# Neighbourhood attention on one Trainium2 core: the order of the opening's transfers

## The chip, the cores and the metric

The kernel runs on one core of one Trainium2 chip. The metric is the device time of one execution in microseconds (us); the time of a kernel is the median of several runs.

## The reference

An image of 224 x 224 positions with 192 channels is projected to queries, keys and values. Every position attends to a 7 x 7 neighbourhood with dilation 2, clipped at the image's edges, with one head of 192 channels. The result is projected by `wo`.

```python
def reference(x, wqkv, wo):
    B, H, W, C = x.shape          # 1, 224, 224, 192, bfloat16
    ks, dil = (7, 2)
    qkv = x @ wqkv
    q, k, v = ...                 # C channels each
    half = (ks - 1) // 2 * dil
    r0 = jnp.clip(ir - half, 0, H - 1 - (ks - 1) * dil)
    c0 = jnp.clip(ic - half, 0, W - 1 - (ks - 1) * dil)
    ...                           # nidx: the 49 neighbours r0 + 2a, c0 + 2b of each position
    logits = jnp.einsum('bnc,bnkc->bnk', qf, kn) * C ** (-0.5)
    p = softmax(logits)
    o = jnp.einsum('bnk,bnkc->bnc', p, vn) @ wo
    return o.reshape(B, H, W, C)
```

## The kernel before, in words

**Two parities, fourteen bands, 28 steps.** With dilation 2 even and odd rows never meet, nor do even and odd columns. A row parity is called `rc`, a column parity `cc`. The image is cut into bands of 16 rows. A step (`rc`, `j`) handles eight query rows of one parity. The steps are run in the order (0,0), (0,1), (1,0), (0,2), (1,1), (0,3) and so on; `si` counts them from 0. A step has seven groups, `t` = 0 to 6.

**Folding.** Queries are not formed by themselves. The product of the query and key weights is folded once at the start, and `g_piece` (L353, L361) applies it to the query rows of a step, in three pieces (kinds 0, 1, 2), into `ga` and `gb`. The value weights are folded with the output weights in the same way: `w_transpose(2, wv, 0)` (L231) transposes the value weights, and `fold_wo` (L243, L244, L269) multiplies them with the output weights into `WP`. So the attention sums raw input rows, and `o_mm` (L447) applies `WP` at the end.

**Three copies of the input.** `load_xt` (L92) brings a band as a transposed copy `xt`, in four parts of four rows, by DMA transposes that SP issues. `key_copy` (L277, L279) rearranges it into the keys `xa` and `xb`; `edge_item` (L295, L303) computes what is special at the image's left and right edge, and `edge_copies` (L329 to L332) puts that into `ga` and `gb`. `load_xn` (L105) brings the rows a second time, not transposed, as values `xn`: one DMA for each of 14 column tiles `n`, band and row parity, into 64 partitions. Two consecutive bands fill the 128 partitions; an even band is in the lower half. `grp_copy` (L208, L210) fills fixed columns beside each value tile, used by one of the two y products.

**A group.** `s_group` (L410, L411) forms scores of four tiles, ACT takes the exponential (L414), and `y_unit` (L429, L435) multiplies the probabilities with value tiles, in pairs of units for a column parity and a half, (`cc`, `h`); the half `h` = 1 uses tiles 7 to 13, and `h` = 0 the tiles from 0 up. `Y0` says in which group of step 0 each unit runs. `o_mm` and `o_out` (L447, L451, L462) of the step before are run between. The order on every engine is written out by hand, as the program's order.

**What step 0 needs.** Step 0 uses band 0 alone. Its groups 3, 4 and 5 form the pieces of step 1, which need parts 0, 1 and 2 of band 1; group 6 runs the edge item of band 1. Step 1 forms the pieces of step 2, of bands 0 and 1; step 2 those of step 3, of bands 1 and 2.

**Queues.** SP issues its transfers in the order of the program. In the program's instructions every transfer that SP issues waits for the end of the eighth one before it (the first weights, issued by ACT, count as the first), and POOL's likewise among themselves. `gate` (L216) is a copy of one element on POOL: it holds back what POOL issues behind it until a given part of a band has landed. `DOWN` is the list of tiles from 13 to 0. Before the change SP issues band 0, two parts of band 1, the value and output weights (L113 to L115), part 2, three value tiles, part 3, seven value tiles of band 1, band 2, and five value tiles of the second parity; POOL issues the other value tiles in one sequence.

Of the kernel before, what the change touches and what calls it, by code (L numbers as in the profile page):

```python
# [17 lines left out]
KC = 8  # L18
QW = KC + HALO
NEG = -30000.0  # L20
XP = 448
# [6 lines left out]
def kernel(  # L28
# [7 lines left out]
    nc = tc.nc  # L36
# [3 lines left out]
    NJ = H // 16  # L40
# [43 lines left out]
    xt = {}  # L84

    def load_xt(b, part):
        if not 0 <= b < NJ:
            return
        if b not in xt:
            xt[b] = xt_pool.tile([128, 3, 16, S], BF, name=f"xt{b}", tag="xt")  # L90
        r = 4 * part
        nc.sync.dma_start_transpose(out=xt[b][:, :, r:r + 4, :].rearrange("p t r c -> p t (r c)"),  # L92
                                    in_=xp[16 * b + r:16 * b + r + 4].rearrange("r j c -> (r j) c"))

    NX = 11
    DOWN = list(range(NK - 1, -1, -1))

    def load_xn(eng, rc, m, tiles):

        if not 0 <= m < NJ:  # L100
            return
        p0 = 64 * (m % 2)
        r0 = 16 * m + rc
        for n in tiles:
            eng.dma_start(out=XN[rc][p0:p0 + 64, XP * n + 64:XP * (n + 1)],  # L105
                          in_=xp[r0:r0 + 15:2, KC * n:KC * (n + 1), :])

    nc.scalar.dma_start(out=wqk[:], in_=wqkv[:, 0:2 * C].rearrange("(a p) c -> p a c", p=CH))
    for part in range(4):
        load_xt(0, part)  # L110
    for part in range(2):
        load_xt(1, part)
    nc.sync.dma_start(out=wv[:], in_=wqkv[:, 2 * C:3 * C].rearrange("(a p) c -> p a c", p=CH))  # L113
    nc.sync.dma_start(out=wo_lo[:], in_=wo[0:128, :])
    nc.sync.dma_start(out=wo_hi[:], in_=wo[64:192, :])  # L115
    load_xt(1, 2)
    load_xn(nc.sync, 0, 0, DOWN[NX:])
    load_xt(1, 3)
    load_xn(nc.sync, 0, 1, DOWN[:7])
    for part in range(4):  # L120
        load_xt(2, part)
    load_xn(nc.sync, 1, 1, DOWN[:5])


    i_id = const.tile([128, 128], I32, name="i_id")
# [75 lines left out]
    def masks(eng, gi, ccs=(0, 1)):  # L201
        for cc in ccs:
            g = GB[gorder[gi] + (cc,)]
            eng.tensor_copy(out=g[CROW[cc]], in_=cmE[CROW[cc]])
            eng.tensor_copy(out=g[RROW[cc]], in_=rm[RROW[cc], gi, :].unsqueeze(1).to_broadcast([32, S, BR]))

    def grp_copy(eng, rc):
        eng(out=XN[rc][:, 0:NK * XP].rearrange("p (n c) -> p n c", c=XP)[:, :, 0:64],  # L208
            in_=grp[:].unsqueeze(1).to_broadcast([128, NK, 64]))
        eng(out=XN[rc][:, NK * XP:], in_=grp[:])  # L210
# [3 lines left out]

    gate = const.tile([1, 1], BF, name="gate")
    nc.gpsimd.tensor_copy(out=gate[:], in_=xt[0][0:1, 0, 12, 0:1])  # L216
    load_xn(nc.gpsimd, 0, 0, DOWN[:NX])


    def filler(n):  # L220
# [5 lines left out]
    def w_transpose(X, src, c0):  # L226
        pool_, tag = (ps_y, "y") if X < 2 else (ps_s, "s")
        tp = pool_.tile([128, 2, 2, CH], BF, name="tp" + tag, tag=tag)
        for i, d0 in enumerate((0, 64)):
            for a in range(2):  # L230
                nc.tensor.transpose(tp[:, i, a, :], src[:, a, c0 + d0:c0 + d0 + 128], ident[0:CH, 0:CH])  # L231
        f = "p a b -> p (a b)"
        nc.scalar.copy(out=wT_lo[:, X, PAD:PAD + C], in_=tp[:, 0].rearrange(f))
        nc.scalar.copy(out=wT_hi[64:128, X, PAD:PAD + C], in_=tp[64:128, 1].rearrange(f))
# [29 lines left out]
    def fold_wo():  # L264
        for kt, cs in enumerate(((64, 0), (-64, 128))):
            pt = ps_y.tile([128, 2, 256], F32, name="prW", tag="y")
            for cc in range(2):
                times(pt[:, cc, 0:C], 2, cs[cc], wo_lo[:], wo_hi[:])
            nc.scalar.copy(out=WP[:, :, kt, 0:C], in_=pt[:, :, 0:C])  # L269
# [118 lines left out]

    yplan = [(0, 1, (2, 3)), (0, 0, (4, 5)), (1, 1, (6, 7)), (1, 0, (8, 8))]
    HS = ((0, H0), (H0, S))  # L390
    Y0 = {(0, 1): (4, 5), (0, 0): (6, 6), (1, 1): (7, 7), (1, 0): (8, 9)}

    class Step:
        pass
# [137 lines left out]
    for si, st in enumerate(steps):  # L532
        rc, j = st.rc, st.j
        prev = steps[si - 1] if si else None
        nxt = steps[si + 1] if si + 1 < len(steps) else None
        st.ysb = [work.tile([128, 2, NO, 128], BF, name=f"ysb{cc}", tag=f"ysb{cc}", bufs=2) for cc in range(2)]

        for (cc, h, ts) in yplan:
            for kt in range(2):
                pend.append((si * T + (ts[kt] if si else Y0[cc, h][kt]), st, cc, h, kt))  # L540
        up = None if si < 2 else (prev.rc, prev.j + 1 + prev.rc)
        if up:
            key_copy(*up, 0, nc.vector.tensor_copy, nc.vector.tensor_copy)
        for t in range(T):
            s_group(st, t)
            if t == (6 if si == 1 else 3) and rc == 0 and 2 <= j + 1 < NJ:
                edge_item(j + 1)
            if si == 0:
                if t == 0:
                    rest(nc.vector.tensor_copy)  # L550
                    g_piece(0, 0, 2)
                    edge_item(0)
                    key_copy(0, 0, 1, nc.vector.tensor_copy, nc.vector.tensor_copy)
                    load_xn(nc.gpsimd, 0, 1, DOWN[7:])
                    load_xn(nc.gpsimd, 1, 0, DOWN[:7])
                    load_xn(nc.gpsimd, 1, 1, DOWN[5:7])
                    load_xn(nc.gpsimd, 1, 0, DOWN[7:])
                    load_xn(nc.gpsimd, 1, 1, DOWN[7:])
                elif t == 1:
                    edge_copies(0, 0, nc.vector)  # L560
                    masks(nc.vector, 2)
                elif t == 2:
                    for cc in range(2):
                        onehots(nc.vector, cc, 1)
                        key_copy(1, 0, cc, nc.vector.tensor_copy, nc.vector.tensor_copy)
                elif t < 6:
                    if t == 3:
                        w_transpose(2, wv, 0)
                    if t == 4:
                        fold_wo()  # L570
                    g_piece(nxt.rc, nxt.j, t - 3)
                else:
                    edge_item(1)
                    edge_copies(nxt.rc, nxt.j, nc.vector)
            elif t < 3 and nxt is not None:
                g_piece(nxt.rc, nxt.j, t)
            if prev is not None:
                tp_ = t - (3 if nxt is not None else 2)
                if 0 <= tp_ < 4:
                    o_out(*o_mm(prev, PIECES[tp_]))  # L580
            run_y(si * T + t)
            if t == (0 if si > 2 else 2) and si > 0 and nxt is not None:
                edge_copies(nxt.rc, nxt.j, nc.gpsimd if si > 1 else nc.vector)
            if up and t == 0:
                load_xn(nc.sync, *up, (12, 11))
                load_xn(nc.gpsimd, *up, (10, 9, 8))
            elif up and t == 1:
                load_xn(nc.gpsimd, *up, (13, 7, 6, 5, 4, 3, 2, 1, 0))
            if nxt is None and t == 4:
                store(prev, [nc.sync, nc.gpsimd], parts=(1, 2))  # L590
            if nxt is None and t == 6:
                first = o_mm(st, (0, 1, 2, 3), (0,))
            if t == 5 and up:
                key_copy(*up, 1, nc.scalar.copy, nc.vector.tensor_copy)

            if si == 1 and t in (0, 2, 4, 5):
                load_xt(3, (0, 2, 4, 5).index(t))
            elif si > 1 and t in (1, 4):
                load_xt(j + (4 if rc else 2), 2 * (rc == 0) + (t == 4))
            if si == 0 and t in (4, 5):  # L600
                key_copy(0, 1, t - 4, nc.vector.tensor_copy, nc.vector.tensor_copy)
            if si == 1:
                if t == 1:
                    masks(nc.vector, 1)
                    grp_copy(nc.scalar.copy, 1)
                if t in (0, 2):
                    key_copy(1, 1, t // 2, nc.vector.tensor_copy, nc.vector.tensor_copy)
            if si > 1 and held and t in (1, 2, 3, 5, 6):
                (nc.sync if t in (2, 5) else nc.gpsimd).dma_start(**held.pop(0))
            if t == 2 and si in (2, 3, 8):  # L610
                masks(nc.vector, {2: 4, 3: 3, 8: 5}[si])
        if prev is not None:
            if si == 1:
                store(prev, None, later=held)
            elif nxt is not None:
                store(prev, [nc.sync])
            else:
                store(prev, [nc.sync, nc.gpsimd], parts=(0, 3), cols=(0, NO))
# [63 lines left out]
```

## Time and profile before

| | |
|---|---|
| median of 3 runs | 328.31 us (328.27 to 328.81) |
| profiled execution | 327.94 us, of which the span is 326.2 us |
| granted TensorE clock, mean | 0.984 |
| busy: PE, DVE, ACT, POOL | 94%, 83%, 76%, 66% of the span |
| moved by DMA | 59.02 MB, 181 GB/s on average |
| first scores of steps 1 and 2 | 28.94 and 41.90 us |

Times in the views count from the span's start. PE is TensorE, PEld its weight loads, DVE VectorE, ACT ScalarE, POOL GpSimd, SP the engine that issues most transfers. A line of a timeline has the start, the duration, the engine, the line of the kernel, what is written and read, and in square brackets how long the engine was idle before and what released it.

### The profile page before, as it was taken

To read this page: it belongs to the slowest core of one execution; us is meant where nothing else is said; L and a number is where in the kernel's file an instruction comes from. 1 tells how busy PE (TensorE), PEld (TensorE's weight loads), DVE (VectorE), ACT (ScalarE), POOL (GpSimd) and SP (SyncE) were. 2 spreads that over 40 slices of the span, in tenths; PEclk is the share of its full clock that TensorE was granted. 3 is DMA by queue.
4 is the path that set the end of the run, shared out by engine and by line. 5 is a ranking of instruction groups with operands and counts; after the bars stand their busy time and mean duration, and the time that the engine had idled before them with its cause. 6 is when DMAs were issued, how large, how long until landed. Compare 5 with 4: busy or idle time off the path is not lost.

```text
span 326.2 us, 12220 instructions
## 1 busy us (share of the span) xinstructions
PE 307.6 (94%) x4978; PEld 270.6 (83%) x4978; DVE 269.3 (83%) x538; ACT 246.9 (76%) x516; POOL 214.6 (66%) x442
## 2 busy tenths in 40 slices
PE   7859999999999999999999999999999999999980
PEld 6537888988889888988899888988899888988980
DVE  8838989988978989888988898788988898887771
ACT  5636777788887787878888787878787887888651
POOL 2768657989766866776668667676567866753052
PEclk9969999999999999999999999999999999999997
DMA  8999999899888999999989998999999943644233
GB/s 162 183 171 179 215 164 220 184 225 225 186 204 209 212 148 199 224 212 210 202 183 205 217 182 161 226 213 184 213 193 207 214 118 105 171 134 124 59 103 97
DMA packets 106319, 59.02 MB, mean 181 GB/s; under 512 B 92945, under 2 KB 100315, under 8 KB 106263
## 3 DMA queue, kind: packets, MB, share of 16 engines
q1 hardware_dynamic: 89479, 40.73, 65.3%
q0 software_dynamic: 16576, 17.37, 22.6%
q8 instruction: 39, 0.64, 0.8%
q10 hardware_dynamic: 208, 0.15, 0.2%
q14 instruction: 17, 0.14, 0.1%
HBM read 19.59 MB, written 19.27 MB: 119 GB/s over the span
## 4 chain that ended last, share of the span: by engine, by line
PE 73%; DVE 14%; SPq 4%; issue 3%; DMA 3%; ACT 1%; POOL 0%; POOLq 0%; DVEq 0%; ACTq 0%
PE y L429 19%; PE po L447 15%; PE pg L353 14%; PE s_ps L410 9%; PE s_ps L411 9%; DVE o_sb L462 6%; PE pg L361 4%; SPq L92 3%; DVE ysb L435 3%; DMA xt<-in_x_dram 2%; PE pe L295 1%; DVE rs L451 1%; DVE gb L367 1%; DVE gb L370 1%; DMA xn<-in_x_dram 1%
## 5 line engine op out<-in xcount | busy, mean ns | idle before, releaser
L105 POOL DMA_DIRECT2D xn<-in_x_dram x329 | 184.8, 587 | 77.0 <-PE y L429 46.0
L414 ACT ACTIVATE p_sb<-s_ps 128x448 bf16<-128x448 f32 (+3 forms) x196 | 105.6, 539 | 20.5 <-PE s_ps L411 20.2
L429 PE MATMUL y<-p_sb,xn 128*128 128x112 bf16 (+5 forms) x1736 | 108.0, 207 | 0.1
L429 PEld LDWEIGHTS <-xn 128*128 128x128 bf16 (+1 forms) x1736 | 95.3, 97 | 13.0 <-issue 6.1
L435 ACT CAST ysb<-y 128x504 bf16<-128x504 f32 (+1 forms) x140 | 73.2, 544 | 35.3 <-PE y L429 32.3
L410 PE MATMUL s_ps<-ga,xa 128*128 128x112 bf16 (+4 forms) x812 | 98.9, 210 | 0.8 <-DVE xa L277 0.5
L411 PE MATMUL s_ps<-gb,xb 128*128 128x112 bf16 (+4 forms) x812 | 98.5, 210 | 0.5 <-DVE gb L330 0.4
L462 DVE TENSOR_TENSOR o_sb<-po,rs 128x768 bf16<-128x768 f32 x109 | 93.5, 858 | 5.3 <-DVE rs L451 0.9
L447 PE MATMUL po<-WP,ysb 128*128 128x193 bf16 x770 | 82.7, 247 | 1.8 <-ACT ysb L435 0.6
L411 PEld LDWEIGHTS <-xb 128*128 128x128 bf16 (+1 forms) x812 | 76.2, 98 | 0.7 <-issue 0.3
L410 PEld LDWEIGHTS <-xa 128*128 128x128 bf16 (+1 forms) x812 | 72.9, 98 | 2.3 <-issue 1.2
L447 PEld LDWEIGHTS <-ysb 128*128 128x128 bf16 x784 | 62.6, 98 | 3.6 <-ACT ysb L435 1.9
L353 PE MATMUL pg<-xt,wz 128*128 128x327 bf16 (+3 forms) x336 | 51.5, 289 | 4.7 <-DMA xt<-in_x_dram 4.6
L435 DVE CAST ysb<-y 128x392 bf16<-128x392 f32 (+1 forms) x84 | 49.6, 591 | 0.9 <-PE y L429 0.7
L451 DVE RECIPROCAL rs<-po 128x4 f32<-128x4 f32 x110 | 19.3, 175 | 21.0 <-PE po L447 19.4
L367 DVE CAST gb<-pg 64x872 bf16<-64x872 f32 x27 | 28.6, 1058 | 7.8 <-PE pg L361 6.9
L353 PEld LDWEIGHTS <-wz 128*128 128x128 bf16 x336 | 24.5, 98 | 12.6 <-issue 4.2
L365 ACT CAST ga<-pg 128x872 bf16<-128x872 f32 x28 | 24.8, 885 | 11.8 <-PE pg L353 11.8
L370 DVE CAST gb<-pg 64x848 bf16<-64x848 f32 x28 | 29.3, 1045 | 0.4
L375 ACT CAST ga<-pg 128x848 bf16<-128x848 f32 x28 | 24.2, 865 | 0.6 <-PE pg L353 0.6
L279 DVE COPY xb<-xt 64x896 bf16<-64x896 bf16 x56 | 23.0, 411 | 0.8
L277 ACT COPY xa<-xt 128x896 bf16<-128x896 bf16 x24 | 22.6, 940 | 0.0
(88 smaller groups left out, 176.7 us busy)
## 6 DMA issues: line engine op xcount, KB each, us to landing
xn<-in_x_dram POOLq DMA_DIRECT2D x329, 48.0 KB, 4.4
out_dram<-o_sb SPq DMA_DIRECT2D x25, 630.0 KB
xn<-in_x_dram SPq DMA_DIRECT2D x63, 48.0 KB
xt<-in_x_dram SPq DMA_TRANSPOSE x56
out_dram<-o_sb SPq DMA_DIRECT2D x50, 9.0 KB
out_dram<-o_sb POOLq DMA_DIRECT2D x9, 78.8 KB, 4.3
out_dram<-o_sb SPq DMA_DIRECT2D x7, 78.8 KB
out_dram<-o_sb SPq DMA_DIRECT2D x25, 18.0 KB
```

Source lines behind the costliest of these rows:

```text
L105: eng.dma_start(out=XN[rc][p0:p0 + 64, XP * n + 64:XP * (n + 1)], in_=xp[r0:r0 + 15:2, KC * n:KC * (n + 1), :])
L353: nc.tensor.matmul(pg[:, a_:b_, 0:nq], lhsT=AW[w], rhs=xt[b][:, k, la:la + 2 * (b_ - a_ - 1) + 1:2, q0:q0 + nq], start=(a_ == ra if kind = ...
L365: nc.scalar.copy(out=A[0][:, 3:S, :], in_=pg[:, :, 0:nq].rearrange(v))
L367: mid(out=Bt[0][0:64, 3:S, :], in_=pg[0:64, :, 0:nq].rearrange(v))
L370: mid(out=Bt[1][64:128, HALO:S, :], in_=pg[64:128, :, 3:nq].rearrange(v))
L410: nc.tensor.matmul(o, lhsT=XA[rc][:, cc, n, 0:kn], rhs=a[:, lo:hi, :].rearrange(f), start=True, stop=False)
L411: nc.tensor.matmul(o, lhsT=XB[cc][rc][:, n, 0:kn], rhs=b_[:, lo:hi, :].rearrange(f), start=False, stop=True)
L414: nc.scalar.activation(out=p[0:kn, 0:off], in_=s_ps[0:kn, 0:off], func=ACTF.Exp)
L429: nc.tensor.matmul(y[:, BR * (a_ - h0):BR * (b_ - h0)], lhsT=XN[st.rc][kp, d:d + 128], rhs=p[kp, off + BR * (a_ - lo):off + BR * (b_ - lo) ...
L435: eng(out=o, in_=y[:, 0:BR * (h1 - h0)].rearrange("p (i n r) -> p i n r", n=NO, r=BR))
L447: nc.tensor.matmul(po[:, k, 0:C + 1], lhsT=st.ysb[cc][:, kt, n, :], rhs=WP[:, cc, kt, 0:C + 1], start=(kt == 0), stop=(kt == 1))
L462: nc.vector.tensor_tensor(out=o, in0=po[:, 0:k, 0:C], in1=rs[:, 0:k].to_broadcast([128, k, C]), op=ALU.mult)
```

## The change

SP issues all four parts of band 1 behind band 0. The value rows of six tiles are then loaded for both bands at once by `load_both`, one DMA into 128 partitions, and only then the weights of values and output; after them band 2 and four tiles of the second parity, again for two bands at once. POOL loads eight tiles of band 0, eight of band 1, waits for the first part of band 2, and loads ten tiles of the second parity for two bands at once. Transposing and folding the output weights go from groups 3 and 4 of step 0 to groups 0 and 1 of step 1. The edge item of band 2 goes from group 6 of step 1 to group 1 of step 2. The first y unit of step 0 goes from group 4 to group 5, beside the second. The `grp_copy` of the second parity goes from group 1 to group 5 of step 1.

```diff
+    def load_both(eng, rc, tiles):
+        for n in tiles:
+            eng.dma_start(out=XN[rc][:, XP * n + 64:XP * (n + 1)], in_=xp[rc:rc + 31:2, KC * n:KC * (n + 1), :])
...
-    for part in range(2):
+    for part in range(4):
         load_xt(1, part)
+    load_both(nc.sync, 0, DOWN[8:])
     nc.sync.dma_start(out=wv[:], in_=wqkv[:, 2 * C:3 * C].rearrange("(a p) c -> p a c", p=CH))
     nc.sync.dma_start(out=wo_lo[:], in_=wo[0:128, :])
     nc.sync.dma_start(out=wo_hi[:], in_=wo[64:192, :])
-    load_xt(1, 2)
-    load_xn(nc.sync, 0, 0, DOWN[NX:])
-    load_xt(1, 3)
-    load_xn(nc.sync, 0, 1, DOWN[:7])
     for part in range(4):
         load_xt(2, part)
-    load_xn(nc.sync, 1, 1, DOWN[:5])
+    load_both(nc.sync, 1, DOWN[10:])
...
-    load_xn(nc.gpsimd, 0, 0, DOWN[:NX])        # NX = 11
+    load_xn(nc.gpsimd, 0, 0, DOWN[:8])
...
-    Y0 = {(0, 1): (4, 5), (0, 0): (6, 6), (1, 1): (7, 7), (1, 0): (8, 9)}
+    Y0 = {(0, 1): (5, 5), (0, 0): (6, 6), (1, 1): (7, 7), (1, 0): (8, 9)}
...
-            if t == (6 if si == 1 else 3) and rc == 0 and 2 <= j + 1 < NJ:
+            if (si, t) == (2, 1):
+                edge_item(2)
+            if t == 3 and rc == 0 and 3 <= j + 1 < NJ:
                 edge_item(j + 1)
...                                            # step 0, group 0
-                    load_xn(nc.gpsimd, 0, 1, DOWN[7:])
-                    load_xn(nc.gpsimd, 1, 0, DOWN[:7])
-                    load_xn(nc.gpsimd, 1, 1, DOWN[5:7])
-                    load_xn(nc.gpsimd, 1, 0, DOWN[7:])
-                    load_xn(nc.gpsimd, 1, 1, DOWN[7:])
+                    load_xn(nc.gpsimd, 0, 1, DOWN[:8])
+                    nc.gpsimd.tensor_copy(out=gate[:], in_=xt[2][0:1, 0, 0, 0:1])
+                    load_both(nc.gpsimd, 1, DOWN[:10])
...                                            # step 0, groups 3 to 5
-                    if t == 3:
-                        w_transpose(2, wv, 0)
-                    if t == 4:
-                        fold_wo()
                     g_piece(nxt.rc, nxt.j, t - 3)
...                                            # later steps, groups 0 to 2
+                if (si, t) == (1, 0):
+                    w_transpose(2, wv, 0)
+                if (si, t) == (1, 1):
+                    fold_wo()
                 g_piece(nxt.rc, nxt.j, t)
...                                            # step 1
                 if t == 1:
                     masks(nc.vector, 1)
+                if t == 5:
                     grp_copy(nc.scalar.copy, 1)
```

## Prediction

> **What bounds the kernel now.** I read the page first, then the opening through the chain of waits, TensorE's timeline, the windows and the queues. In the page, PE is busy for 94% of the span; the two weak places are the first and the last slices.
>
> ```profile
> PE   7859999999999999999999999999999999999980
> PEclk9969999999999999999999999999999999999997
> DMA  8999999899888999999989998999999943644233
> ```
>
> Slice 3 (16.3 to 24.5 us) is the only place before the tail where PE is half idle and its granted clock falls; DMA is full from the start. The chain of waits, restricted to 12 to 24 us, says which transfer:
>
> ```profile
> 11.63 0.43 SPq L114
> 12.06 0.04 issue
> 12.11 0.43 SPq L115
> 12.54 0.04 issue
> 12.58 7.33 DMA xt<-in_x_dram
> ```
>
> Columns are start, duration, what. SP issues the two copies of the output weights, then band 1's part 2, which lands 7.33 us later, at 19.91. TensorE's timeline shows who waits, and the windows what its clock does:
>
> ```profile
> 15.38 0.34 PE L231 MATMUL tps<-ident,wv 96*128 96x96 bf16 x4
> 15.56 0.54 PE L353 MATMUL pg<-xt,wz 128*128 128x327 bf16 x4
> 19.95 0.89 PE L353 MATMUL pg<-xt,wz 128*128 128x436 bf16 x2 [3.85 <-DMA xt<-in_x_dram]
> ...
> 15.23:18.64 3.41, 0.87 (x11) 0.53 (x9) 3.34 (x9) 1.05 (x3) 2.34 (x4) 1.00 1.08 132
> 18.64:22.06 3.42, 2.10 (x13) 1.23 (x13) 0.62 (x2) 1.18 (x2) 2.70 (x6) 0.51 1.26 195
> 22.06:25.47 3.41, 3.41 (x25) 2.14 (x24) 0.69 (x1) 1.23 (x4) 2.18 (x5) 0.50 0.80 163
> ```
>
> In a window line the first "us, (x)" pair is PE, and the three figures at the end are clock, DMA share, GB/s. PE idles 3.85 us; the clock is 1.00 to 18.64, then half until 25.47, two stretches of 3.41 us. VectorE waits with it, and later becomes the bound itself:
>
> ```profile
> 24.77 1.06 DVE L367 CAST gb<-pg 64x872 bf16<-64x872 f32 x1 [5.50 <-PE pg L361]
> 32.45 1.06 DVE L367 CAST gb<-pg 64x872 bf16<-64x872 f32 x1
> ```
>
> From 32.45 the chain runs on DVE to 41.21, and later again. Both were released by PE, so an earlier PE moves this chain too. After 70 us no wait of PE on a DMA appears among its waits and its steps are about 11 us, nearly all busy: what the opening gains should reach the end.
>
> **DMA prices.** A half tile of value rows (48 KB): page section 3 has q0 move 17.37 MB in 22.6% of 326.2 us, 4.24 us a MB, so 0.21 us. A both-band tile is counted twice that, 0.42. A part of a band (344 KB transposed): q1's 65.3% are 213 us for 40.73 MB; 21.4 MB of that are stores and straight loads, 91 us at q0's price, leaving 122 us for 56 parts, 2.2 us each. Bounds: band 0's four parts landed at 10.32 (POOL's gate), of which about 2.0 are start and 0.6 the first weights, hence 1.93; and part 2 to part 3 of band 1 took 3.84 us (19.91 to 23.75, when SP's queue ends its 0.9 us wait), beside three half tiles from SP and about 4.5 from POOL, hence 2.27. The three later weight transfers have 448 rows of 384 bytes; the first weights took 0.6 us with 208 packets, so 1.3 us; the rest of the wait for part 3 (10.32 to 23.75, less 4 x 2.2 and 14 x 0.21) bounds it above by 1.7.
>
> **Part 2 earlier.** In the changed order it has no weights ahead: 10.32 + 3 x 2.2 + five POOL half tiles (POOL's lane waits show about one landing per us from 12 on) x 0.21 = 18.0 (17.1 to 18.4). PE arrives 0.18 earlier, as the value-weight transposes are gone from this spot, so it idles about 2.1 us instead of 3.85.
>
> **The clock.** The stretch to 18.64 would be 0.7 + 0.6 = 1.3 of 3.41 busy, 38%. Before it was 26% and the clock fell; a stretch at 68% (315.65 to 319.07) kept it. 38% lies nearer to 26%, so I take a fall, and because the next stretch is full, recovery at 22.06: half the former penalty. The Trainium skill ("TensorE: Matmul & The Clock Gate", HAM oscillation) says instead that only idle gaps over about 3.4 us matter; the trace disagrees in part, for the fall came 2.5 us after PE's last matmul. By that rule there would be no fall, PE would reach the next data 1.7 us sooner, and the early-tile rival below would follow.
>
> **Rest of step 0.** From 19.95 to step 1's first scores at 28.94 PE did 5.52/2 + 3.47 = 6.2 us of full-clock work; without the folding (21.66 to 22.92 at half clock, 0.63) 5.6. The last 0.9 is the pair of y units of (0,0), now the first users of the tiles that SP loads for both bands. From 18.0 PE gets there at 22.7 at full clock, at 24.4 with the fall. y of (0,1), moved a group later, needs POOL's first seven half tiles; the seventh lands by about 20.5, PE gets there at 20.8: free. The edge item needs part 3: 18.0 + 2.2 + 0.6 = 20.8, free too.
>
> **Tile 0** is the last of SP's six both-band tiles and the first that y of (0,0) reads. After part 3: 6 x 0.42, and about six POOL half tiles beside it, 1.3: 24.6. Bounds: 22.1 with 1.93 per part and three half tiles, 26.2 with 2.27 and all sixteen of POOL's landed. SP's issue is no limit: part 3 ends its issue near 14.3, six issues at 0.65 end near 18.3, and each waits for the eighth transfer before it, the last for band 1's part 1. So y of (0,0) starts at 24.6 whichever way the clock goes, and step 1 at 25.5 instead of 28.94: 3.4 earlier.
>
> **Moved work.** Value-weight transposes (0.18) and folding (0.63) now run in step 1's first two groups: +0.8 on PE. Behind them on PE wait the key-map pieces, which feed the DVE chain. The weights land behind tile 0 at 25.2 to 26.0; PE asks for them at 26.0 and 28.3: covered, and worth up to 1 if not. ACT's four copies (0.30, 0.31, 0.48, 0.48) come where the two group copies of the second parity (0.94, 0.25) leave; those go to group 5, where ACT had idle of 0.4 to 0.8 us per group. The folding shares the y banks, whose evictions fall before it: zero, bound 0.5. The step-1 edge item (0.46 on PE, 0.47 on DVE) goes to step 2, and with it the 0.55 wait that followed (40.71 to 41.26, on a normalization freeing its bank); DVE is nearly full in step 2 too, so I count half: -0.3, bounds 0 and -0.6.
>
> **Queues behind.** POOL's new gate waits for band 2's part 0 (tile 0 at 24.6, weights 1.3, 2.2, a little POOL: about 28.5); behind it stand ten both-band tiles of the second parity. At POOL's 0.57 us an issue (1.1 if it grew with the partitions) the seventh goes out at 32.5 (36.2) and lands 5 us later, 37.5 (41); step 2's first y, at 46.56 before, comes near 43.7. Band 2's part 3 lands at 28.5 + 3 x 2.2 + up to 4.2 = 35 to 39; DVE's key copy, at 42.75 before, comes near 39.9. Both covered, the second closely. Fewer DMA instructions (20 tiles at double width) shorten only issue queues: nothing.
>
> Sum: -3.4 + 0.8 - 0.3 = -2.9 on the profiled 327.94, 325.0. The median of before is 0.37 above that execution, so 325.4. About 0.2% (0.66 us) is what a measurement tells from no change.
>
> **Rivals.**
> Tiles early: if tile 0 lands near 22.7 and the clock holds, step 1 starts at 23.6; -5.3 + 0.8 - 0.3 = -4.8, 323.5. For it: DMA shares of 1.2 to 1.5 in 12 to 20 us show overlap that my unit prices omit. Against: it needs the low end of two bounds and an untested clock. 0.14.
> The stall moves: all transfers share the same engines, already full (share 0.8 to 1.6 from 4 us on), so what is postponed is late next. Counting to the end of the second parity's first tiles: 12 x 2.2 + 56 x 0.21 + 0.6 + 1.3 + 2.0 = 42.1, beside up to four parts of band 3; step 2's second y pair comes at about 46. A stall there, or at the key copy, of 1 to 2 us leaves a gain near 1.4: 326.9. The Trainium skill ("DMA: Bandwidth & Descriptors", Issuing engines are not separate DMA queues) says of sharing what these rows show. 0.16.
> Nothing: part 2 lands at 19.9 as before, the weights having filled gaps; then only small shifts remain, 328.2. 0.06.
> Slower: the clock holds at 18.64, PE reaches y of (0,0) at 22.7, and tile 0 comes only at 27. PE is then idle 2.8 of the 3.41 us to 25.47, the clock falls there, stays half through the partly idle next stretch to 28.88 and up to 32.3. The two y units end at 28.8, and 1.75 us are lost to the slow clock; with +0.8 and -0.3 that is 28.8 - 28.9 + 1.75 + 0.5 = +2.1, 330.4. It decides from tile 0 at about 26, my upper bound. 0.14, with unknown waits of this kind.
>
> **Numbers.** Forecast 0.50, as above, its own range 324.0 to 326.3. Faster: 0.50 + 0.14 + 0.16 = 0.80; same 0.06; slower 0.14. The range leaves out the slower case and the ends of the others: 323.2 to 328.2.
>
> **What would show it.** Right: PE's wait for band 1 ends near 18; half clock for one stretch or none before 23; a wait of y on value rows near 24.6; step 1's scores at 25.5; L367 of step 1 about 2.4 us earlier than 32.45; no PE wait on DMA later. Wrong: part 2 landing after 19, tile 0 after 26, a clock fall at 25.47, or a DVE key copy waiting for band 2 in step 2.

## Result: 1.1% slower, though TensorE finishes earlier

The changed kernel takes 331.75 us (median of six runs, 330.52 to 332.29) beside 328.18 us of the kernel before (six runs, 327.5 to 328.81): a ratio of 1.0106, 95% interval 1.0083 to 1.0129. The forecast was 325.4. The profiled execution took 332.1 us with a span of 330.2 us; before, 327.94 and 326.2.

The opening first. From the page of the changed kernel, the rows of PE, its granted clock and DMA over 40 slices:

```profile
PE   7779999999999999999999999999999999999930
PEclk9979999999999999999999999999999999999985
DMA  9999999989998999999998889989898654442350
```

The weak third slice has become better on PE. At the other end PE's slice 39 has fallen from 8 to 3, though its work is the same: the span goes on for longer after TensorE has stopped. The chain of waits of the changed kernel (start, duration, what), its PE timeline and its windows at the places that the prediction showed:

```profile
9.51 1.66 SPq L92
11.17 0.04 issue
11.21 7.65 DMA xt<-in_x_dram
```

```profile
18.91 0.92 PE L354 MATMUL pg<-xt,wz 128*128 128x436 bf16 x2 [2.80 <-DMA xt<-in_x_dram]
...
25.25 1.22 PE L430 MATMUL y<-p_sb,xn 64*128 64x112 bf16 x16
26.40 0.20 PE L411 MATMUL s_ps<-ga,xa 128*128 128x64 bf16 x1
...
26.93 0.92 PE L354 MATMUL pg<-xt,wz 128*128 128x436 bf16 x6
```

```profile
15.51:18.92 3.41, 0.61 (x8) 0.33 (x6) 3.34 (x9) 0.54 (x1) 1.25 (x2) 1.00 1.24 158
18.92:22.33 3.41, 3.41 (x21) 1.69 (x22) 0.42 (x2) 1.42 (x2) 3.21 (x6) 0.50 1.13 281
22.33:25.74 3.41, 3.41 (x58) 2.69 (x56) 3.21 (x5) 2.21 (x4) 0.11 (x1) 1.00 1.21 209
```

Part 2 of band 1 has no weights ahead of it and lands at 18.9, so PE idles 2.80 us instead of 3.85. The clock is half for one stretch (18.92 to 22.33) instead of two. The y products of (0,0) at 25.25 have no bracket: they wait for no value rows. Step 1's first scores come at 26.40, 2.5 us earlier. VectorE's key-map copy of step 1, which began at 32.45 before:

```profile
31.46 1.06 DVE L368 CAST gb<-pg 64x872 bf16<-64x872 f32 x1 [1.43 <-PE pg L362]
```

Of the 2.5 us, 1.0 is left here. From step 2 on, the second piece of each step starts 1.3 to 1.6 us earlier than before, to the last; ACT's last work ends at 318.26 instead of 319.66, and the last store lands at 322.22 instead of 323.94.

So the whole loss, and more, lies behind the last landing. There each engine ends with DRAIN instructions, and POOL's longest DRAIN, called the drain below, is what changes. The instructions of the program's last line (engine, operation, count: shortest, median and longest in ns, first and last start), before and after:

```profile
L677 POOLq DRAIN  x3: 40/102/4627, 320.5 to 325.9; - x3
L677 SPq DRAIN  x3: 7/7/13, 325.3 to 325.7; - x3
```

```profile
L679 POOLq DRAIN  x3: 40/102/10308, 319.1 to 330.0; - x3
L679 SPq DRAIN  x3: 7/7/13, 323.4 to 329.7; - x3
```

And SP's waits between 300 us and the end (us in total, times, longest), before and after:

```profile
SPq L677 <- DMA out_dram<-o_sb: 3.2, 3, 2.6
SPq L677 <- PEq L677: 0.7, 2, 0.5
```

```profile
SPq L679 <- PEq L679: 6.7, 2, 6.2
SPq L679 <- DMA out_dram<-o_sb: 2.6, 3, 1.6
```

Before, SP's last long wait is for the stores. After, it has seen the stores land and waits 6.2 us more for the other engines at the common end (the view puts PE's name to it; PE's own drains last 1.3 us at most, and the late one is POOL's). POOL's drain takes 10.31 us instead of 4.63. It ends 7.2 us after the last store has landed, instead of 1.2. The account: the landing 1.7 us earlier, the drain's end 6.0 us later behind it, 4.3 in all, of which the span shows 4.0 (326.2 to 330.2).

### The profile page after: what moved, and what is told of

The parts are those of the page before. It is cut to its first block, busy times and chain, and to the rows that moved or that the text cites. A ratio compares the mean times of both kernels' runs of the same rounds, so it can differ in the third digit from the quotient of the medians.

```text
span 330.2 us, 12196 instructions
## 1 busy us (share of the span) xinstructions
PE 307.4 (93%) x4978; PEld 270.2 (82%) x4978; DVE 269.6 (82%) x538; ACT 247.0 (75%) x516; POOL 205.4 (62%) x428
## 4 chain that ended last, share of the span: by engine, by line
PE 73%; DVE 14%; SPq 3%; issue 3%; DMA 2%; ACT 1%; POOL 0%; POOLq 0%; DVEq 0%; ACTq 0%
PE y L430 19%; PE po L448 16%; PE pg L354 14%; PE s_ps L411 9%; PE s_ps L412 9%; DVE o_sb L463 5%; PE pg L362 4%; SPq L92 3%; DVE ysb L436 2%; DMA xt<-in_x_dram 2%; PE pe L296 1%; DVE gb L368 1%; DVE gb L371 1%; DVE rs L452 1%; DVE gb L205 1%
## 5 line engine op out<-in xcount | busy, mean ns | idle before, releaser
L104 POOL DMA_DIRECT2D xn<-in_x_dram x304 | 170.4, 588 | 75.9 <-PE y L430 42.1
L354 PE MATMUL pg<-xt,wz 128*128 128x327 bf16 (+3 forms) x336 | 51.6, 289 | 4.1 <-DMA xt<-in_x_dram 4.1
L354 PEld LDWEIGHTS <-wz 128*128 128x128 bf16 x336 | 24.4, 98 | 12.2 <-DMA xt<-in_x_dram 3.7
L368 DVE CAST gb<-pg 64x872 bf16<-64x872 f32 x27 | 28.6, 1058 | 6.3 <-PE pg L362 5.5
```

What stands on the lines that cost most here:

```text
L354: nc.tensor.matmul(pg[:, a_:b_, 0:nq], lhsT=AW[w], rhs=xt[b][:, k, la:la + 2 * (b_ - a_ - 1) + 1:2, q0:q0 + nq], start=(a_ == ra if kind = ...
L368: mid(out=Bt[0][0:64, 3:S, :], in_=pg[0:64, :, 0:nq].rearrange(v))
```

## Experiments

The change takes 15 transfers off POOL (352 become 337): ten tiles for two bands replace twenty half tiles, and five go to SP. The experiments ask what of this makes the drain long. "Transfers" below are those that POOL issues.

### Form or count: halves, before_337, after_352

`halves` is the changed kernel with the ten both-band tiles of POOL as twenty half tiles again (347 transfers):

```diff
-                    load_both(nc.gpsimd, 1, DOWN[:10])
+                    load_xn(nc.gpsimd, 1, 0, DOWN[:10])
+                    load_xn(nc.gpsimd, 1, 1, DOWN[:10])
```

> The changed kernel, but POOL loads the ten tiles of the second parity as twenty half tiles (64 partitions each), so that no POOL transfer has 128 partitions; POOL issues 347 transfers in all (changed kernel 337, before 352). Theory 'form': the 10.3 us of POOL's last DRAIN comes from the 128-partition transfers; then the drain falls to about 4.6 us and the time to about 326.5. Theory 'count': the drain follows the number of POOL transfers; it changes with 347, to a value not known beforehand. Theory 'gate': the second copy on POOL between transfers is what is paid; drain stays near 10 us, time 332.

`before_337` is the kernel before, with fifteen half tiles of steps 8 to 14 issued by SP instead of POOL; `after_352` is the changed kernel with fifteen of steps 8 to 15 issued by POOL instead of SP:

```diff
-                load_xn(nc.sync, *up, (12, 11))
-                load_xn(nc.gpsimd, *up, (10, 9, 8))
+                few = {8: 3}.get(si, 2 if 9 <= si <= 14 else 0)          # before_337
+                load_xn(nc.sync, *up, (12, 11) + (10, 9, 8)[:few])
+                load_xn(nc.gpsimd, *up, (10, 9, 8)[few:])
...
+                more = {8: 1}.get(si, 2 if 9 <= si <= 15 else 0)         # after_352
+                load_xn(nc.sync, *up, (12, 11)[more:])
+                load_xn(nc.gpsimd, *up, (12, 11)[:more] + (10, 9, 8))
```

> The kernel before, with 15 half tiles of steps 8 to 14 issued by SP instead of POOL: POOL issues 337 transfers, as in the changed kernel, but all in the old form and with the old opening. 'Count': drain near 10.3 us and a time near 333.5, slower than before by over 5 us though nothing else changes. 'Form' and 'gate': drain stays at 4.6 us, time 328.

> The changed kernel, with 15 half tiles of steps 8 to 15 issued by POOL instead of SP: POOL issues 352 transfers, as before. 'Count': drain back at 4.6 us and the time near 326.5, faster than before by 1.4 to 1.9. 'Form' and 'gate': drain stays near 10 us, time 332.

Measured: `halves` has a drain of 4.18 us and takes 326.54 us, 0.9945 of before (0.9916 to 0.9974), as theory 'form' had it. But `after_352` keeps the both-band tiles and has a drain of 4.50 us; its time, 327.74 us, 0.9995 (0.9966 to 1.0025), misses the 326.5 that 'count' expected. `before_337` has the old opening and a drain of 10.31, 338.66 us, 1.0315 (1.0252 to 1.0378). So the form of the transfers does not do it, nor the new opening; the number does something. `before_337` was a poor instrument for the price: it also lost 7 to 8 us between 139 and 209 us, where PE waited up to 2.65 us at a time for value rows, now partly from SP's queue. Right behind the longest of these waits the granted clock was half for one stretch (167.8 to 171.2 us).

### Neither the second gate nor the program's length: nogate, pad_337

`nogate` takes the second `gate` copy out of the changed kernel. `pad_337` puts fifteen one-element writes on POOL at the start:

```diff
-                    nc.gpsimd.tensor_copy(out=gate[:], in_=xt[2][0:1, 0, 0, 0:1])      # nogate
...
+    for _ in range(15):                                                                # pad_337
+        nc.gpsimd.memset(gate[:], 0.0)
```

> The changed kernel without the copy on POOL that waits for band 2's first part, so that POOL issues the second parity's tiles without that wait; 337 transfers. 'Gate': drain back to 4.6 us, time near 326.5, or more if the tiles now delay band 2. 'Count' and 'form': drain near 10 us, time 332 or more.

> The changed kernel with fifteen one-element memsets more on POOL, where it waits for band 0 anyway: 337 POOL transfers, but as many POOL instructions (448) as the 352-transfer kernel. If the drain follows the number of transfers it stays at 10.31 us and the time near 331.5. If it follows the length of POOL's program it falls to about 4.5 us and the time to about 326.

Both keep a drain of 10.31 us: 331.38 us, 1.0126 (1.0083 to 1.0169), and 331.49 us, 1.0108 (1.0063 to 1.0153). The gate, which the prediction had looked at for what stands behind it, costs nothing that these runs show.

### A wrong turn: a remainder, a threshold, an event

`after_338` and `after_353` move one and sixteen half tiles from SP to POOL, by the edit of `after_352`; `after_327` has SP issue the ten held stores (stores of the opening's results, which POOL otherwise issues in steps 2 and 3); `after_342` moves five half tiles to POOL.

```diff
-                (nc.sync if t in (2, 5) else nc.gpsimd).dma_start(**held.pop(0))
+                nc.sync.dma_start(**held.pop(0))                                       # after_327
```

> The changed kernel with one half tile of step 8 on POOL instead of SP: 338 transfers, 434 instructions. A threshold between 337 and 347: drain most likely still 10.31 us, time near 331.5. A remainder (of 8 or 16, say) that only 337 has: drain at 4.5 us, time near 326.

> The changed kernel with sixteen half tiles of steps 8 to 15 on POOL instead of SP: 353 transfers, with the same remainder by 8 and 16 as 337. A threshold: drain 4.5 us, time near 327. A remainder by 8 or 16: drain 10.31 us, time near 332.

> The changed kernel, with the ten stores of steps 0 that POOL issues in steps 2 and 3 issued by SP instead: POOL issues 327 transfers. In the kernels with 347, 352 and 353 transfers POOL pauses 2.4 to 2.6 us, waiting for nothing shown, after exactly its 332nd transfer. Theory 'event': something costly follows the 332nd transfer, hidden when it lies before the last loads and paid in the last DRAIN when it lies among the last stores (337, 338). Then with 327 it is never reached: no pause, drain about 4.5 us, time near 326. Theory 'threshold' (few transfers, long drain): drain 10.31 us, time near 331.5.

> The changed kernel with five half tiles of steps 8 to 10 on POOL instead of SP: 342 transfers, the 332nd is the third of the thirteen last stores, some 6 us before the drain begins. 'Event': between 4.5 and 10.3 us of drain, long if the event is only worked off at the end, and a time of 327 to 332. 'Threshold between 338 and 347': either.

Measured: drains of 10.39 (338), 4.38 (353), 10.06 (327) and 2.46 us (342); times of 332.13, 1.0128 (1.0095 to 1.0161); 327.31, 0.9988 (0.9964 to 1.0013); 331.81, 1.0123 (1.0076 to 1.0169); 326.32, 0.9981 (0.9943 to 1.0019). No remainder decides, and the theory that too few transfers would spare the work altogether fell with `after_327`. What was left looked like a threshold between 338 and 342. One row of `after_342` did not fit two states: its drain is shorter than that of any other kernel, and POOL pauses among the last stores. From POOL's timeline:

```profile
318.88 1.17 POOL L501 DMA_DIRECT2D out_dram<-o_sb  x2 [3.17 <-issue]
```

### The count alone falls: before_337b

The kernel before with 337 transfers again, but so that TensorE should not wait: the held stores by SP as in `after_327`, and one half tile to SP in each of five steps far apart.

```diff
+                few = 1 if si in (10, 13, 16, 19, 22) else 0
+                load_xn(nc.sync, *up, (12, 11) + (10, 9, 8)[:few])
+                load_xn(nc.gpsimd, *up, (10, 9, 8)[few:])
```

> The kernel before, with 337 instead of 352 transfers on POOL as in the changed kernel, but taken off POOL so that TensorE should not wait: the ten held stores of the early steps are issued by SP, and one half tile of value rows in each of the steps 10, 13, 16, 19 and 22. Theory 'count' (with few transfers POOL pays at the end what it otherwise pays in a pause within the run): POOL's last drain near 10.3 us instead of 4.6, no pause after its 332nd transfer, the other work as before, so about +5.7 us: 333.5 to 334.5, ratio near 1.018. Rival 'opening' (the long drain belongs to the new opening, and the earlier kernel with 337 transfers lost its time to SP's late tiles): drain near 4.6 and a time of 327.5 to 329.

The drain takes 2.79 us with 337 transfers, and the time is 328.99 us, 1.0044 (1.002 to 1.0068). 'Count' missed both; 'opening' has the time within its range, but neither the drain of 2.79 nor the 10.31 that the old opening had in `before_337`. POOL's timeline has, after its 219th and its 329th transfer:

```profile
206.09 4.42 POOL L105 DMA_DIRECT2D xn<-in_x_dram  x8 [2.47 <-issue]
318.90 2.77 POOL L475 DMA_DIRECT2D out_dram<-o_sb  x5 [2.35 <-issue]
```

These pauses, in which POOL waits for nothing that the profile shows, had been in the trace of before all along:

```profile
104.67 1.68 POOL L105 DMA_DIRECT2D xn<-in_x_dram  x3 [2.10 <-issue]
198.47 2.77 POOL L105 DMA_DIRECT2D xn<-in_x_dram  x5 [2.15 <-issue]
292.01 3.88 POOL L105 DMA_DIRECT2D xn<-in_x_dram  x7 [2.36 <-issue]
```

They follow the 120th, the 226th and the 332nd transfer: 106 between each two. The changed kernel has the first two alone:

```profile
119.39 6.66 POOL L104 DMA_DIRECT2D xn<-in_x_dram  x12 [4.62 <-PE s_ps L412]
211.31 1.17 POOL L104 DMA_DIRECT2D xn<-in_x_dram  x2 [4.34 <-issue]
```

Its first one is put down to PE, as in several other runs: a wait for something else falls into the same place. But in all seventeen profiles POOL stops for 1.77 us or more at each of the places, and no stop of over 1.3 us that is put down to nothing stands ahead of any other transfer. In the kernels whose held stores SP issues, they follow the 113th and the 219th, again 106 apart. Ten stores move the place by seven, so a store counts for about 0.3 of a value-row transfer (and the first pause comes after 113 by this count); a both-band tile counts like a half tile, since `after` and `halves` both pause after the 226th. With that count every run falls into place: `after_342` has 103 value rows and 10 stores from its 226th transfer to the 339th, 106, and pauses there; `before_337b` has 105 and 5, 106.5; the changed kernel has 98 and 13, 102, and ends before the next pause is due; `after_338` has 103.

### Since the last pause: after_385, after_315

The new theory: what POOL does in a pause is left to the last drain for the transfers since the last pause. All runs so far had at most 12 of them or at least 99. `after_385` gives POOL all of SP's later half tiles, `after_315` gives SP one more in each later step.

```diff
+                more = 2 if si <= 26 else 0                                            # after_385
+                load_xn(nc.sync, *up, (12, 11)[more:])
+                load_xn(nc.gpsimd, *up, (12, 11)[:more] + (10, 9, 8))
...
+                few = 1 if 4 <= si <= 26 else 0                                        # after_315
+                load_xn(nc.sync, *up, (12, 11) + (10, 9, 8)[:few])
+                load_xn(nc.gpsimd, *up, (10, 9, 8)[few:])
```

> The changed kernel with all of SP's later half tiles issued by POOL: 385 transfers. Theory 'since the last pause': POOL pauses about 2.4 us after each 106 value-row transfers (a store counts for 0.3), and the last drain has to do what piled up since the last pause. Here the last pause falls after the 332nd transfer, 40 value rows and 13 stores follow, 44 by that count; with 0.08 us for each below the 102 and 10.31 us of the changed kernel the drain takes 5.7 us (6.6 by the line between 352's 4.6 at 11 and 327's 10.06 at 99). The end comes 1 to 2 us later than with 342 to 353 transfers: 328 to 330, if POOL's extra issuing costs nothing else. Rival 'two states' (short from 342 transfers on): drain 4.2 to 4.6.

> The changed kernel with one half tile a step moved from POOL to SP in the later steps: 315 transfers. Theory 'since the last pause': the last pause falls after the 226th transfer, 76 value rows and 13 stores follow, 80 by that count: drain 8.5 us (8.9 by the other line), so about 1.5 us less than the changed kernel at the end, 330, if SP's extra issuing costs nothing else. Rival 'two states': drain 10.0 to 10.4 as with 327 to 338.

The last line's rows, `after_385` and then `after_315`:

```profile
L680 POOLq DRAIN  x3: 40/93/5702, 332.1 to 338.3; - x3
```

```profile
L680 POOLq DRAIN  x3: 40/102/8512, 322.6 to 331.6; - x3
```

5.70 and 8.51 us, where 5.7 and 8.5 were expected and two states would have given 4.4 and 10.2. The drain by what follows the last pause (value rows, and stores at 0.3):

| since the last pause | kernels | drain, us | its end behind the last landing, us |
|---|---|---|---|
| 1 and 2 | after_342, before_337b | 2.46, 2.79 | 0.8, 1.0 |
| 6 | halves, halves_fold | 4.18, 4.23 | 1.1 |
| 11 and 12 | before, after_352, fold_late_352; after_353 | 4.63, 4.50, 4.63; 4.38 | 1.2 to 1.3 |
| 44 | after_385 | 5.70 | 2.6 |
| 80 | after_315 | 8.51 | 5.4 |
| 99 | after_327, fold_late_327 | 10.06, 10.06 | 6.9, 7.2 |
| 102 | after, nogate, pad_337, before_337 | 10.31 | 7.2 for after |
| 103 | after_338 | 10.39 | 7.0 |

From 44 up a line through the rows is 2.2 + 0.08 x count. The short drains do not follow it: they all end 0.8 to 1.3 us behind the last landing, which suggests that the stores set the end there. A drain lies beside the last stores for some 4.5 us (4.63 in before), so by the line, as an estimate, about 28 transfers since the last pause cost nothing, and each further one 0.08 us. The line also says that the drain is not simply the pause put off: 106 transfers would add 8.5 us to a drain, and a pause takes mostly 2.1 to 2.7. What makes the drain so much dearer stays open.

As times both runs missed, for the extra issuing did cost something else. `after_385` took 340.08 us, 1.0384 (1.0345 to 1.0423): PE waited 11.8 us in mid-run for value rows, now all on POOL's queue. `after_315` took 333.73 us, 1.0206 (1.0162 to 1.025): one step from 221.7 to 236.2 us lasted 3.8 us longer than in the others. PE waits 2.2 us there, until 227.0, for a half tile that SP issued at 222.2, so for one of those that the edit moved, and not for a transfer behind POOL's pause (222.3 to 224.7). PE was 36% busy in that stretch of 3.41 us, and in the next one, though full, its clock was half:

```profile
224.26:227.67 3.41, 1.24 (x25) 1.00 (x24) 0.62 (x1) 1.63 (x4) 2.93 (x6) 1.00 0.91 156
227.67:231.09 3.42, 3.42 (x40) 3.31 (x38) 1.92 (x5) 0.83 (x3) 3.03 (x7) 0.50 1.11 256
```

A stretch of 3.41 us at half clock does about 1.7 us less work, which would be the rest of the 3.8.

### The folding's place: fold_late_352, fold_late_327, halves_fold

In the changed kernel the folding stands ahead of step 1's second piece, in accumulator banks that y products share. PE's waits around it, and the chain of waits there:

```profile
29.36 0.24 PE L244 MATMUL prW<-wo_lo,wz 128*128 128x192 bf16 x1 [0.16 <-DVE ysb L436]
30.06 0.24 PE L244 MATMUL prW<-wo_lo,wz 128*128 128x192 bf16 x1 [0.21 <-ACT ysb L436]
```

```profile
28.73 0.52 ACT ga L366
29.25 0.27 issue
29.52 0.50 ACT ysb L436
30.06 0.24 PE prW L244
```

The folding waits for VectorE and then for ACT to evict a y bank, ACT is itself behind with the transposed weights and the key map, and the piece that feeds VectorE stands behind the folding. These runs put it behind the piece and the y unit of that group; 352, 327 and 347 transfers are made by the edits of `after_352`, `after_327` and `halves`.

```diff
-                if (si, t) == (1, 1):
-                    fold_wo()
                 g_piece(nxt.rc, nxt.j, t)
...
             run_y(si * T + t)
+            if (si, t) == (1, 1):
+                fold_wo()
```

> The changed kernel with 352 POOL transfers, and the folding behind the group's key-map piece and y unit instead of ahead of them (step 1, group 1). Theory 'banks': in the changed kernel the folding waits for evictions of the y banks and holds up the key-map piece, and with it VectorE's chain, by about 1 us more than its own 0.65; then the cast of that piece starts 1 us or more earlier against the piece before it, and the time falls by 1.0 to 1.6 below the 352-transfer kernel, to about 326. Rival, DVE bound anyway: no change.

> Both: the changed kernel with the folding behind the piece and 327 POOL transfers. 'Event' and 'banks': 325 or a little below, the fastest of all; 'threshold': 330.5.

> The changed kernel with the second parity's ten tiles as twenty half tiles on POOL (347 transfers) and the folding behind the piece and the y unit of step 1's group 1: the two edits that each gave the lowest times so far, together. If their gains add (0.9945 and 0.9969 against about 0.999 for the new opening with the short drain): near 0.993, 325.5. If the time is bounded in the steps behind by the value rows' transfers (an earlier TensorE waits for them): no more than either alone, 0.994 to 0.999. Drain 4.2 to 4.6, with a pause after POOL's 332nd transfer.

The time from the second piece in step 0 to that in step 1 (the first products L354 with `m`) was 9.6 to 10.4 us in the kernels of this opening without the edit (11.5 in `after_315`), and 8.4, 8.7 and 9.4 with it: worth about 1 us there. None of it is clear at the end. `fold_late_352` takes 326.98 us, 0.9969 (0.9934 to 1.0003), where about 326 was expected; `fold_late_327` 332.93, 1.0154 (1.01 to 1.0208), with its drain of 10.06, where 325 or 330.5 were expected; and `halves_fold` 327.46, 0.9991 (0.9972 to 1.001), where the two best edits together are no better than `halves` alone. Part of where it may have gone shows in the profile of `fold_late_352`, in PE's waits between 60 and 320 us:

```profile
PE y L430 <- DMA xn<-in_x_dram: 2.6, 2, 1.8
```

Before has no such wait after 70 us. It appears in the profiles of `halves` (0.8 us), `after_353` (1.5) and `fold_late_327` (2.1) too, but not in `halves_fold`, whose profiled execution is its fastest (325.0; its runs go up to 328.51). Why one such kernel's runs spread over as much as 5.0 us (324.75 to 329.77 for `fold_late_352`) or 6.8 us (324.61 to 331.39 for `halves`), where those of before spread over 2.7 us in the same set at most, stays open.

## Why the prediction was wrong, by its steps

**The step that failed** is "Fewer DMA instructions (20 tiles at double width) shorten only issue queues: nothing". Fifteen transfers less on POOL put the third pause past the program's end and left 102 transfers to the last drain: +6.0 us behind the last landing. No rival had it; the slower case had its place at tile 0 and the clock, and neither occurred. Of the four signs of being wrong that it named, none appeared either. The prediction read the tail only as a weak slice of PE. Its sentence "what the opening gains should reach the end" held to the last store (1.7 us earlier) and not to the program's end. Had the drain ended 1.1 us behind the landing, the profiled execution would have taken 332.1 - 6.1 = 326.0 us.

**Part 2 at 18.0** (17.1 to 18.4): 18.9 here, 17.3 to 19.7 in the thirteen other profiles with the new order, 18.4 on average over the fourteen; the old order gave 19.95, 19.21 and 19.48. Right in kind, but a gain of 1.1 us on average rather than 1.9: the 19.91 that it was counted from is the latest of the three.

**The clock**: one stretch at half, as forecast, but after a stretch that was 18% busy instead of 38%. PE's idle time before it was 2.80 us, so the rule of 3.4 us that the prediction set beside its own did not hold here; in `pad_337` the clock fell with 1.30 us of idle time, behind a stretch that was 55% busy. The prediction's guess that 38% is too little is borne out: in all seventeen profiles every stretch at most 43% busy was followed by half clock. Of the thirteen other profiles five had two, and `after_315` had its one only at 26.3; without that one, the first began anywhere from 16.8 to 19.3. The prediction took the place of the stretches from one profile, so that it got one stretch is in part luck.

**Tile 0** at 24.6: its semaphore has its last update at 24.43 in the trace, so the landing was right. But it did not set the start: y of (0,0) came at 25.25 without a wait, because PE itself got there only then. The prediction had PE there at 24.4; part 2 came 0.9 later than 18.0, and step 1 began 0.9 later than 25.5, at 26.40.

**Moved work, +0.8, the y banks at zero, bound 0.5**: the transposes and the folding were sized right, the banks were not. With 2.5 us gained at step 1's start and 0.8 spent, 1.7 should have been left at L368; 1.0 was. Moved away, the folding's wait gave about 1 us within step 1.

**The edge item, -0.3** (0 to -0.6): from step 1's piece to step 2's took 12.33 us before and 11.78 after, -0.55, within the bounds.

**Queues behind the gate**: no wait of step 2 on value rows or on band 2 appears in the changed kernel, as forecast.

The opening is worth less than the forecast's 2.9 us even without the drain. The six kernels with the new opening and a short drain have ratios of 0.9945 to 0.9995, that is 0.2 to 1.8 us. Their medians (326.3 to 327.7) lie in the forecast's range, but so does the 328.18 of before, so this says little for the forecast. Of these only `halves` is faster than before by more than its interval; as the best of six whose intervals overlap it is flattered, and `halves_fold`, with the same transfers and the folding moved, does not repeat it. What all six show is that the loss was no price of the new order.

## To carry to other kernels

Read the program's end in the profile before you cost a change: which engine's last instruction ends after the last landing, and what it has left to do. Count the transfers that a change takes from or gives to POOL, mark POOL's pauses that wait for nothing, and see how many transfers follow the last one; a few transfers more can be cheaper than a few less. When a time jumps at a threshold, look for a period behind it, and try the middle between the two values that you have.

## What the runs showed of the hardware

In this kernel POOL pauses 1.8 to 3.2 us, mostly 2.1 to 2.7 (longer where a wait for something else falls in with it), after 113 value-row transfers and then after each 106 more, a store counting for about 0.3. Transfers into 64 and into 128 partitions count alike. With 44 to 103 transfers since the last pause POOL's drain takes 2.2 us plus 0.08 us for each of them, 10.4 us at the most seen. The pauses are not set by other instructions on POOL (`pad_337`). What POOL does in the pauses and in the drain was not shown. The Trainium skill ("DMA: Bandwidth & Descriptors", SWDGE vs HWDGE vs iDMA) says that GpSimd writes the descriptors of its transfers to rings. A guess is that space in a ring is taken back when it runs short, and at the end; no run here shows the ring.

The granted clock of TensorE changes in stretches of 3.41 us. In the seventeen profiles each of the 28 stretches at full clock in which PE was at most 43% busy was followed by half clock, and none of those with 56% or more; from 44% to 55% nine were and three were not. So a wait can cost more than its length: behind the 2.2 us wait of `after_315` and the 2.65 us wait of `before_337` (stretches 36% and 22% busy) a full stretch ran at half clock.
